# Running the output projection, LayerNorm and FFN of one query chunk inside the attention of the next, in a pre-norm transformer block

## The chip, the cores and the metric

The kernel runs on one core of a Trainium2 chip. The metric is device time in microseconds (us) of one execution. Runs marked "one look" have one time, no interval and a state that is on record as unknown; they are read by stretches of their traces.

Engines are named as the profile names them: PE (matmul), PEld (weight load of PE), ACT (activations), DVE (vector), SP (which issues the loads). "Granted clock" is the share of full speed at which PE was clocked. PSUM is the memory that matmuls write their sums to, in eight banks. PV is the product of the exps of the scores with V.

## The reference

```python
x = A_x                                     # 1 x 2048 x 1024, bf16
h = x + attention(layernorm(x), wqkv) @ wo  # 32 heads of 32, full softmax over 2048 keys
out = h + (gelu(layernorm(h) @ w1 + b1) @ w2 + b2)   # w1: 1024 x 3584, w2: 3584 x 1024
```

## The kernel before

A small planner records every operation with the buffers that it reads and writes, and turns them into semaphore waits. Each engine runs its own list strictly in the order of recording. So the order in which Python records the operations is the order on PE, and an operation that has to wait holds back all behind it.

The kernel has three stages, one after the other: LayerNorm with the Q, K and V projections; attention for all four query chunks of 512; then the output projection (Wo), the second LayerNorm and the FFN for all four chunks.

Attention handles one *unit* per exp: two heads of a group of four, one key tile of 128. Cut to its core:

```python
def stage_A(hu):       # scores: two matmuls with 32 rows each, side by side in the array
    for j in range(2):
        pe(matmul(sT[:, s, j, :], KT[32*hl:32*hl+32, g, keys], QT[32*hl:32*hl+32, g, queries],
                  tile_position=(32*hl, 0)))
def stage_B(hu):       # one exp on ACT over both: 128 x 1024
    act(activation(PT[:, ps], sT[:, s], Exp, bias=..., scale=SCALE))
def stage_C(hu1):      # every second unit: 4 PV and 4 denominator matmuls, 32 columns each
    for hl in range(4): pe(matmul(OTp[32*hl:32*hl+32, oi], Vsb[...], PT[...], tile_position=(0, 32*hl)))
    for hl in range(4): pe(matmul(DENp[32*hl:32*hl+32, oi], ones32, PT[...], tile_position=(0, 32*hl)))

LA = NSTP              # 2: score tiles in PSUM, so two units of lookahead
for hu in range(NHU):
    if hu + LA < NHU:
        stage_A(hu + LA); stage_B(hu + LA)
    if hu % 2 == 1:
        stage_C(hu)
        if last_key_tile: finish_group(qc, g)    # reciprocal of DENp, times OTp
```

`[... the projections, the third stage with eight PSUM banks, W2 streamed once per chunk, all cut]`

## Time and profile before

The median is 1943.18 us (4 runs, 1941.04 to 1944.95).

| stage | us of the span | what bounds it |
|---|---|---|
| LayerNorm 1, projections | 0 to 248 | PE, clock 0.96 |
| attention, 4 chunks of 277 us | 248 to 1358 | ACT, with PE nearly full at clock 0.50 |
| Wo, LayerNorm 2, FFN | 1358 to 1939 | PE, clock 0.90, and gaps |

First, lines of the page of the kernel before. The digits are busy tenths in 40 slices of the span; PEclk is the granted clock in the same slices. The two groups name the tile written and read, the shapes, the count, then busy time, the mean of one in ns, and the idle time before them.

```profile
span 1939.2 us, 24118 instructions
PE   4889989999999999999999999999489789779798
ACT  3433389999999999999999999999246045054060
PEclk9999955555555555555555555555689889889899
...
L527 ACT ACTIVATE PT<-sT,biasm 128x1024 bf16<-128x1024 f32 x1024 | 1058.0, 1110 | 51.1 <-PE sT L516 51.1
L516 PE MATMUL sT<-QT,KT 32*128 32x512 bf16 x2048 | 593.4, 603 | 54.8 <-ACT PT L527 54.1
```

ACT idles 51 us in 1024 exps, so the exps set the pace of attention; PE, at half clock, idles little more (55 us at its score matmuls). The clock falls to half at the start of attention and stays there.

Next, four stretches of the kernel before: length, busy time of each engine with the count of instructions, then the granted clock, the share of the DMA engines and GB/s.

```profile
core 0: us, PE busy (x) PEld busy (x) DVE busy (x) ACT busy (x) POOL busy (x), PEclk, DMA share, GB/s
0.00:248.00 248.00, 202.60 (x964) 92.28 (x964) 116.12 (x285) 91.99 (x134) 1.04 (x9) 0.96 0.37 119
248.00:525.00 277.00, 261.58 (x1520) 43.85 (x1524) 28.35 (x14) 264.36 (x257) 0.00 (x0) 0.51 0.00 1
525.00:1358.00 833.00, 794.05 (x4616) 132.63 (x4608) 97.20 (x48) 794.52 (x770) 0.00 (x0) 0.50 0.00 1
1358.00:1939.00 581.00, 478.98 (x2216) 215.73 (x2216) 265.58 (x502) 196.47 (x301) 0.00 (x0) 0.90 0.39 120
```

In the last 581 us ACT works 196 us. Last, PE's instructions in order of time within attention: start, length, then what it is. One period of two exps goes from 801.46 to 803.47, 2.01 us; the next takes 2.32 us, with a wait of 0.20 us for an exp, and so on in turn, which makes the mean of 2.17 us. "x4" at 802.97 is two score pairs in a row, the second at 803.47.

```profile
801.46 0.61 PE L516 MATMUL sT<-QT,KT 32*128 32x512 bf16 x2 [0.20 <-ACT PT L527]
802.00 0.62 PE L544 MATMUL OTp<-PT,Vsb 128*32 128x512 bf16 x4
802.40 0.64 PE L552 MATMUL DENp<-PT,ones 128*32 128x512 bf16 x4
802.97 1.11 PE L516 MATMUL sT<-QT,KT 32*128 32x512 bf16 x4
```

Tiled matmuls that start together occupy PE for one *slot*: 0.40 us from PV to denominators. From a score pair to PV the distance is 0.54 us and from the denominators to a score pair 0.57 us. Those two steps change the tiling of the array (32-row tiles to 32-column tiles and back); PV to denominators doesn't.

### The profile page before, as it was taken

Reading aid. Unit: us, or ns where it says so; the run is one execution under the profiler, and the core shown is the slowest. Engines: PE = TensorE matmul, PEld = TensorE weight load, DVE = VectorE, ACT = ScalarE, POOL = GpSimd, SP = SyncE. Lnnn points to the kernel's source line nnn. Section 1 sums busy time; section 2 is a strip of 40 time slices with the busy share of each in tenths; the row PEclk is TensorE's granted clock in tenths of the full one; section 3 lists DMA queues with packets and bytes.
Section 4 is the critical chain, followed back from the end, with each engine's and each line's share of the span. In section 5 each row is a group of like instructions: output and inputs, shape, how many; then the busy total and the mean of one; then the engine's idle time right before and its main releaser. Section 6 shows DMA issues by size and latency. Waiting matters only on the chain.

```text
span 1939.2 us, 24118 instructions
## 1 busy us (share of the span) xinstructions
PE 1737.2 (90%) x9312; PEld 484.5 (25%) x9312; DVE 507.2 (26%) x849; ACT 1347.3 (69%) x1458; POOL 1.0 (0%) x9
## 2 busy tenths in 40 slices
PE   4889989999999999999999999999489789779798
PEld 2344411111111111111111111111134334334343
DVE  5443500010100101001010010100356156165281
ACT  3433389999999999999999999999246045054060
POOL 0000000000000000000000000000000000000000
PEclk9999955555555555555555555555689889889899
DMA  4343200000000000000000000000422433523434
GB/s 112 130 150 122 95 1 1 1 1 1 1 1 1 1 1 1 1 1 1 1 1 1 1 1 1 1 1 1 152 66 77 150 121 93 173 82 109 155 127 131
DMA packets 84176, 100.13 MB, mean 52 GB/s; under 512 B 7265, under 2 KB 64609, under 8 KB 84066
## 3 DMA queue, kind: packets, MB, share of 16 engines
q1 hardware_dynamic: 84066, 98.59, 16.2%
q8 instruction: 78, 1.28, 0.3%
q14 instruction: 32, 0.26, 0.0%
HBM read 94.38 MB, written 4.19 MB: 51 GB/s over the span
## 4 chain that ended last, share of the span: by engine, by line
PE 60%; ACT 18%; issue 15%; DVE 4%; DMA 2%; ACTq 0%; SPq 0%; DVEq 0%
PE sT L516 15%; ACT PT L527 15%; PE pb L731 10%; PE pb L701 9%; PE OTp L544 7%; PE DENp L552 6%; PE psq L390 6%; PE pb L656 3%; PE psv L435 3%; ACT xnb L336 1%; DVE l3stats L316 1%; DVE ost L746 1%; DMA w1st<-in_B_w_dram 1%; PE pn L410 1%; ACT xnT L347 1%
## 5 line engine op out<-in xcount | busy, mean ns | idle before, releaser
L527 ACT ACTIVATE PT<-sT,biasm 128x1024 bf16<-128x1024 f32 x1024 | 1058.0, 1110 | 51.1 <-PE sT L516 51.1
L516 PE MATMUL sT<-QT,KT 32*128 32x512 bf16 x2048 | 593.4, 603 | 54.8 <-ACT PT L527 54.1
L563 DVE RECIPROCAL rdenf<-DENp 128x512 f32<-128x512 f32 x32 | 107.5, 3358 | 991.0 <-PE DENp L552 991.0
L552 PE MATMUL DENp<-PT,ones 128*32 128x512 bf16 x2048 | 328.6, 633 | 0.0
L544 PE MATMUL OTp<-PT,Vsb 128*32 128x512 bf16 x2048 | 315.4, 608 | 0.4 <-ACT PT L527 0.4
L516 PEld LDWEIGHTS sT<-QT,KT 32*128 32x128 bf16 x2048 | 105.0, 99 | 710.6 <-ACT PT L527 709.5
L706 ACT ACTIVATE xh<-pb,b1half 128x512 bf16<-128x512 f32 x112 | 76.9, 686 | 244.1 <-PE pb L701 243.9
L701 PE MATMUL pb<-hnT,w1st 128*128 128x512 bf16 x896 | 211.5, 397 | 34.9 <-DMA w1st<-in_B_w_dram 33.7
L731 PE MATMUL pb<-w2st,gT 128*128 128x512 bf16 x896 | 194.4, 379 | 0.0
L390 PE MATMUL psq<-xnT,wst 128*128 128x512 bf16 x512 | 129.6, 401 | 4.8 <-ACT l1y L326 2.4
L701 PEld LDWEIGHTS pb<-hnT,w1st 128*128 128x128 bf16 x896 | 90.4, 102 | 148.6 <-DMA w1st<-in_B_w_dram 35.1
L731 PEld LDWEIGHTS pb<-w2st,gT 128*128 128x128 bf16 x896 | 87.5, 98 | 106.2 <-issue 1.2
L544 PEld LDWEIGHTS OTp<-PT,Vsb 128*32 128x32 bf16 x2048 | 57.3, 102 | 224.5 <-issue 223.2
L711 DVE SCALAR_TENSOR_TENSOR uu<-sqf,xh 128x512 bf16<-128x512 bf16 x112 | 77.5, 692 | 3.8
L687 DVE SCALAR_TENSOR_TENSOR gT<-th,xh 128x512 bf16<-128x512 bf16 x112 | 76.7, 685 | 3.5 <-ACT th L685 3.2
L685 ACT ACTIVATE th<-uu 128x512 bf16<-128x512 bf16 x112 | 69.7, 622 | 3.6 <-DVE uu L711 2.8
L656 PE MATMUL pb<-Wo,OT 128*128 128x512 bf16 x256 | 59.8, 390 | 13.1 <-DMA Wo<-in_A_wo_dram 13.1
L390 PEld LDWEIGHTS psq<-xnT,wst 128*128 128x128 bf16 x512 | 52.1, 102 | 71.8 <-issue 18.3
L746 DVE TENSOR_TENSOR ost<-pb,hch 128x512 bf16<-128x512 f32 x32 | 19.9, 684 | 188.2 <-PE pb L737 188.0
L709 DVE TENSOR_TENSOR sqf<-xh 128x512 bf16<-128x512 bf16 x112 | 47.6, 425 | 64.0 <-ACT xh L706 63.7
L552 PEld LDWEIGHTS DENp<-PT,ones 128*32 128x32 bf16 x2048 | 64.0, 114 | 0.0
L435 PE MATMUL psv<-wst,xnT 128*128 128x512 bf16 x256 | 55.9, 379 | 0.0
(66 smaller groups left out, 490.5 us busy)
## 6 DMA issues: line engine op xcount, KB each, us to landing
w1st<-in_B_w_dram SPq DMA_DIRECT2D x28, 1024.0 KB, 5.5
w2st<-in_B_w_dram SPq DMA_DIRECT2D x112, 256.0 KB, 2.6
wst<-in_A_wqkv_dram SPq DMA_DIRECT2D x24, 1024.0 KB, 5.0
xring<-in_A_x_dram SPq DMA_DIRECT2D x32, 256.0 KB, 4.0
out_dram<-ost SPq DMA_DIRECT2D x32, 128.0 KB, 1.7
Wo<-in_A_wo_dram SPq DMA_DIRECT2D x1, 2048.0 KB, 8.4
b2row<-in_B_b_dram SPq DMA_DIRECT2D x1, 2.0 KB
b1col_bf<-in_B_b_dram SPq DMA_DIRECT2D x1, 7.0 KB, 4.6
```

The source lines that it names most:

```text
L390: pe(lambda p, dc=dc, b=b, s=s, cin=cin, xt=xt: p.matmul(psq[:, b, :], wst[:, s, dc, cin:cin + P], xnT[:, xt, dc, :], start=(dc == 0), sto ...
L435: pe(lambda p, dc=dc, t4=t4, s=s, pvs=pvs, xt=xt: p.matmul(psv[:, pvs, 0:OB], xnT[:, xt, dc, t4 * P:(t4 + 1) * P], wst[:, s, dc, :], start ...
L516: pe(lambda p, s=s, j=j, kt=kt, g=g, hl=hl, qc=qc: p.matmul(sT[:, s, j, :], KT[32 * hl:32 * hl + 32, g, kt * P:(kt + 1) * P], QT[32 * hl:3 ...
L527: act(lambda a, s=s, ps=ps, g=g, qc=qc: a.activation(PT[:, ps, :, :], sT[:, s, :, :], ACT.Exp, bias=biasm[:, g, qc:qc + 1], scale=SCALE), ...
L544: pe(lambda p, j=j, kt=kt, g=g, hl=hl, ps=ps, start=start, stop=stop, oi=oi: p.matmul(OTp[32 * hl:32 * hl + 32, oi, :], Vsb[:, kt, g * P + ...
L552: pe(lambda p, j=j, hl=hl, ps=ps, start=start, stop=stop, oi=oi: p.matmul(DENp[32 * hl:32 * hl + 32, oi, :], ones32[:, :], PT[:, ps, j, :] ...
L563: dve(lambda v, rs=rs, oi=oi: v.reciprocal(rdenf[:, rs, :], DENp[:, oi, :]), reads=[B_DENp[oi]], writes=[B_rdenf[rs]])
L656: pe(lambda p, sa=sa, g=g, qc=qc, t4=t4, j=j: p.matmul(pb[:, sa, 0:OB], OT[:, qc, g, t4 * P:(t4 + 1) * P], Wo[:, g, j * OB:(j + 1) * OB], ...
L701: pe(lambda p, hb=hb, s=s, dc=dc, f4=f4, hn=hn: p.matmul(pb[:, hb, :], w1st[:, s, dc, f4 * P:(f4 + 1) * P], hnT[:, hn, dc, :], start=(dc = ...
L706: act(lambda a, gs=gs, hb=hb, fc=fc: a.activation(xh[:, gs, :], pb[:, hb, :], ACT.Identity, bias=b1half[:, fc:fc + 1], scale=0.5), reads=[ ...
L711: dve(lambda v, gs=gs: v.scalar_tensor_tensor(uu[:, gs, :], sqf[:, gs, :], C1, xh[:, gs, :], ALU.add, ALU.mult), reads=[B_sqf[gs], B_xh[gs ...
L731: pe(lambda p, ci=ci, fc=fc, t4=t4, j=j, s2=s2: p.matmul(pb[:, ci, 0:OB], gT[:, fc, t4 * P:(t4 + 1) * P], w2st[:, s2, j * OB:(j + 1) * OB] ...
```

## The change

The intent is to fill PE's and ACT's unlike loads into one another. The post-attention work of chunk c-1 becomes a generator that yields after about four full 128x512 matmuls (a *slice*; 140 steps a chunk), and the attention loop of chunk c takes a step after 3 of every 5 units. The work of the last chunk has no attention to hide in; it is the *tail*. The rest makes room:

- Q goes out to HBM and comes back one chunk at a time.
- All weights of the post work go through one ring of three 1 MB slots, and PSUM keeps two banks (pbA, pbB) for all the post work. So FFN2 takes two outputs at a time and W2 is streamed four times per chunk.
- Evictions of Wo and FFN1 and the normalization move from ACT to DVE.
- PV and denominators have one bank each in place of two; DVE copies them out before the reciprocal.
- GELU buffers shrink from three to two.
- Buffers track which addresses they reuse, in place of a wait for everything so far.

The cut below is condensed: lines are shortened to their sense.

```diff
+        def post_gen(qc):                      # Wo, LN, transposes, FFN1, FFN2 of one chunk
+            srcs += [(W2 block b) for _ in range(4) for b in range(FC // 4)]     # streamed 4 times
+            ...
+                    for g in range(G):
+                        pe(... pw[:, 0:OB], OT[...], wring[...])                 # Wo into pbA / pbB
+                        if g == G // 2 - 1:
+                            yield
+                    dve(lambda v: v.tensor_copy(attb[:, ab, :], pw[:, 0:OB]))    # was act(... Copy)
+                    ...
+                    dve(lambda v: v.tensor_scalar(xh, pw, 0.5, b1half, MULT, ADD))  # was act(Identity)
+            for ci in range(0, len(combos), 2):                                  # FFN2, 2 banks
+                for fc in range(FC):
+                    ... 2 matmuls ...
+                    if fc % 2 == 1:
+                        yield
+        for qc in range(NCH):
+            for _ in attention_gen(qc):
+                i += 1
+                if post is not None and i % 5 in (0, 2, 4):
+                    next(post)                  # (StopIteration handled)
+            post = post_gen(qc)
-        # attention of all chunks, then:
-        for qc in range(NCH):
-            ffn1_gen(qc) woven with wo_ln_gen(qc + 1)
-            ffn2_plan(qc)                       # 8 PSUM banks, W2 streamed once
```

`[... Q through HBM, buffer tracking, group end: cut]`

## The prediction

> **What bounds it now.** The 40-slice picture shows three stages. LayerNorm and projections take 248 us. Attention runs from 248 to 1358 us (1110 us, 277 us per query chunk). Output projection, LayerNorm and FFN take the last 580 us. In attention the groups view gives 1024 exps of 1.03 us issue spacing (ACT about 95% busy, 51 us idle in all): ACT bounds it. PE also looks 95% busy there, but at granted clock 0.50. In the timeline one period of two exps lasts 2.01 us, in which PE streams four slots (two score pairs, four column-tiled PV, four column-tiled denominator matmuls) of about 0.43 us: 1.7 us. In the last stage PE does 512 full 128x512 matmuls per chunk (plus transposes and bias) at clock 0.91, at 0.216 us each (16 in 3.45 us in the chain of waits), so 110 us per chunk; the rest is LayerNorm, load and eviction gaps. ACT is under 40% busy there.
>
> **What the change does.** It runs the post-attention work of chunk c-1 inside the attention of chunk c, about 140 slices of four full matmuls among 256 exps. Only chunk 3's post work remains as a tail. To make room Q goes through HBM, W2 is streamed four times per chunk (29 MB instead of 7), PSUM accumulators shrink to two banks, and the Wo and FFN1 evictions and the normalization go from ACT to DVE. Denominator and output are copied out by DVE (2 x about 0.69 us per group) before the 3.36 us reciprocal.
>
> **Costing a hidden chunk (estimates).** ACT: 277 us + 28 tanh x 0.62 + 4 hnT copies x 1.02 + 2 table loads x 1.28 = 301 us; with stalls at group boundaries and slice waits about 313 us. The Trainium skill ("ScalarE: Activation LUTs", Table sets) puts exp and tanh in one set, so tanh should not reload; the trace has no exp-tanh alternation to show it. DVE: about 150 us, hidden. DMA: in FFN2 1 MB per about 3.7 us, 285 GB/s; W1 bursts reached 350-380 GB/s here, so it just fits. PE: 110 us post + 128 x 0.86 = 220 us at full clock: fits under ACT. At half clock 219 + 219 us plus mode switches, about 460-480 us: PE would bound.
>
> So the clock decides. The skill ("TensorE: Matmul & The Clock Gate", Part 1) says the clock gate opens on activity, half or full. Here attention stayed at 0.50 for 1100 us after a 2 us gap, while full matmuls opened it within about 5 us. I expect dense full-array slices to open it (about 75-80%), with cold stretches around LayerNorm steps.
>
> **Tail.** Wo 15, LayerNorm 10, transposes 8, FFN1 about 70 (DVE-bound: 0.69+0.43+0.69+0.69 = 2.5 us per block of 8 matmuls), FFN2 about 90 (DMA-bound: 29 MB at about 330 GB/s), ends 7: 200 us.
>
> **Sum.** 248 + 277 + 3 x 313 + 200 = 1664, say 1665 us; range 1600 to 1980. Of the roughly 580 us at the end, about 415 go into attention, which grows by about 110; the tail costs 60 more than a quarter of before. Chances: faster 0.82, same 0.04, slower 0.14.
>
> **What would show it.** Granted clock: 0.5 in the first attention chunk, near 1.0 in chunks 1 to 3; ACT about 90% busy there; exp idle under 15%; no table load per tanh; chunks of about 313 us; a tail of about 200 us with FFN2 waiting on weight loads; W2 traffic about 118 MB.
>
> **What would make it wrong.** The clock stays at 0.5 in the mixed chunks: 460+ us each, total about 2100 us. Or W2 loads block PE in order and so starve exp. Or tanh reloads tables (2 x 1.28 us x 28 per chunk). Or DVE copies at group ends stall the single output bank for several us, 32 times.

## The result, and the profile after

The changed kernel takes 1696.27 us (median of 8 runs, 1691.83 to 1702.17), with an output that passed the comparison (e3_quarter shows what that is worth). The ratio to the kernel before is 0.8733 (95% interval 0.8722 to 0.8744). Ratios in this document are of fast runs of the same rounds, so not quite the ratio of the medians that are quoted.

Lines of the page of the changed kernel, as those of before:

```profile
span 1690.4 us, 24078 instructions
PE   4898889999999899999988999999899999957666
ACT  4334349999998899888988998888899988922200
PEclk9999995555556799999787999996799999779998
...
L654 ACT ACTIVATE PT<-sT,biasm 128x1024 bf16<-128x1024 f32 x1024 | 1074.6, 1117 | 89.3 <-PE sT L643 86.0
L643 PE MATMUL sT<-QTc,KT 32*128 32x512 bf16 x2048 | 447.1, 461 | 66.6 <-ACT PT L654 64.8
```

PEclk is at half in the first attention chunk, then mostly open. A chunk with post work in it is called *mixed* below. Exps idle 89 us in place of 51. The stretches of the changed kernel, cut at the ends of the attention chunks:

```profile
core 0: us, PE busy (x) PEld busy (x) DVE busy (x) ACT busy (x) POOL busy (x), PEclk, DMA share, GB/s
0.00:248.00 248.00, 201.91 (x964) 92.22 (x964) 116.14 (x285) 92.64 (x134) 1.05 (x9) 0.96 0.45 145
248.00:525.00 277.00, 262.23 (x1524) 44.44 (x1524) 37.34 (x28) 264.36 (x257) 0.00 (x0) 0.50 0.04 13
525.00:845.00 320.00, 297.55 (x2104) 82.75 (x2100) 135.11 (x193) 287.93 (x292) 0.00 (x0) 0.92 0.41 132
845.00:1165.00 320.00, 297.76 (x2092) 82.75 (x2088) 135.08 (x193) 287.70 (x291) 0.00 (x0) 0.92 0.41 132
1165.00:1484.00 319.00, 297.64 (x2094) 82.78 (x2091) 135.47 (x194) 289.06 (x292) 0.00 (x0) 0.92 0.40 129
1484.00:1690.00 206.00, 137.60 (x552) 52.44 (x550) 97.42 (x165) 23.22 (x34) 0.00 (x0) 0.91 0.55 182
```

So 581 us of post work turned into about 42 us in each of three chunks and a tail of 206 us. A finer ruler is used from here on: attention ends a *group* of four heads (32 exps) with a DVE copy of its output, and the time between two such copies is the time of a group. A group alone takes 34.7 us in both kernels. In the first mixed chunk the eight take:

| group | 1 | 2 | 3 | 4 | 5 | 6 | 7 | 8 |
|---|---|---|---|---|---|---|---|---|
| post work in it | Wo | LayerNorm, transposes, FFN1 | FFN1 | FFN1 | FFN1, FFN2 | FFN2 | FFN2 | FFN2, none |
| us | 41.3 | 46.0 | 40.4 | 37.4 | 42.0 | 38.0 | 38.1 | 35.4 |

How the clock opened can be seen on PE, in order of time, at the first slice of the first mixed chunk:

```profile
530.83 1.89 PE L751 MATMUL pbA<-wring,OT 128*128 128x512 bf16 x4
532.65 0.56 PE L643 MATMUL sT<-QTc,KT 32*128 32x512 bf16 x4
533.14 0.40 PE L670 MATMUL OTp<-PT,Vsb 128*32 128x512 bf16 x4
533.37 0.39 PE L678 MATMUL DENp<-PT,ones 128*32 128x512 bf16 x4
533.69 1.04 PE L751 MATMUL pbA<-wring,OT 128*128 128x512 bf16 x4
```

The first slice of four took 1.89 us at half clock, the second 1.04 us at full clock; by the clock record it opened at 533.0 us, 2.2 us after the first slice began. In all traces here the recorded clock changes only in steps of about 3.4 us, so such delays are coarse. And this is PE in the FFN2 part of the same chunk:

```profile
715.41 0.39 PE L643 MATMUL sT<-QTc,KT 32*128 32x512 bf16 x2
715.73 0.39 PE L823 MATMUL pbA<-wring,gT 128*128 128x512 bf16 x1
715.96 0.38 PE L823 MATMUL pbB<-wring,gT 128*128 128x512 bf16 x1
...
716.39 0.38 PE L823 MATMUL pbB<-wring,gT 128*128 128x512 bf16 x1
716.70 0.39 PE L643 MATMUL sT<-QTc,KT 32*128 32x512 bf16 x2
717.02 0.40 PE L670 MATMUL OTp<-PT,Vsb 128*32 128x512 bf16 x4
717.25 0.39 PE L678 MATMUL DENp<-PT,ones 128*32 128x512 bf16 x4
717.57 0.39 PE L643 MATMUL sT<-QTc,KT 32*128 32x512 bf16 x2
```

Read the distances of the starts, not the lengths, which include the way through the pipeline. Between matmuls of one tiling it is 0.22 us (715.73 to 715.96; 717.02 to 717.25). Where the tiling changes (score pair to full, full to score pair, score pair to PV, denominators to score pair) it is 0.31 or 0.32 us. Each change costs PE about 0.10 us at full clock, and somewhat more at half clock (0.54 to 0.57 in place of 0.40 from PV to denominators and 0.40 to 0.43 between the full matmuls of the slice at 530.83). The Trainium skill ("TensorEngine Tiling (Array Packing)", Key Properties) says that changing the tiling mode drains the engine; it has no figure, and this is one for this kernel. That a drain is the whole of the 0.10 us is not shown.

### The profile page after: what moved, and what is told of

Same layout as the page of the kernel before. It is cut to its first block, busy times and chain, and to the rows that moved or that the text cites. A ratio compares the mean times of both kernels' runs of the same rounds, so it can differ in the third digit from the quotient of the medians.

```text
span 1690.4 us, 24078 instructions
## 1 busy us (share of the span) xinstructions
PE 1494.7 (88%) x9312; PEld 437.4 (26%) x9312; DVE 656.6 (39%) x1057; ACT 1244.9 (74%) x1298; POOL 1.0 (0%) x9
## 4 chain that ended last, share of the span: by engine, by line
PE 61%; ACT 13%; DVE 11%; issue 10%; DMA 4%; ACTq 0%; DVEq 0%; SPq 0%
PE sT L643 16%; ACT PT L654 11%; PE OTp L670 8%; PE psq L472 6%; PE DENp L678 5%; PE pbA L823 5%; PE pbB L823 5%; PE pbB L792 4%; PE pbA L792 4%; DMA wring<-in_B_w_dram 3%; PE psv L525 3%; DVE rdenf L690 2%; DVE xh L800 2%; DVE uu L805 2%; PE pbA L751 2%
## 5 line engine op out<-in xcount | busy, mean ns | idle before, releaser
L643 PE MATMUL sT<-QTc,KT 32*128 32x512 bf16 x2048 | 447.1, 461 | 66.6 <-ACT PT L654 64.8
L670 PE MATMUL OTp<-PT,Vsb 128*32 128x512 bf16 x2048 | 243.7, 466 | 4.4 <-DVE OT L688 2.5
L678 PE MATMUL DENp<-PT,ones 128*32 128x512 bf16 x2048 | 244.8, 468 | 0.3
L643 PEld LDWEIGHTS sT<-QTc,KT 32*128 32x128 bf16 x2048 | 95.5, 94 | 536.2 <-ACT PT L654 397.3
L823 PE MATMUL pbA<-wring,gT 128*128 128x512 bf16 x448 | 178.6, 399 | 32.0 <-DMA wring<-in_B_w_dram 26.2
L823 PE MATMUL pbB<-wring,gT 128*128 128x512 bf16 x448 | 177.0, 395 | 2.1 <-DVE ost L843 2.1
L792 PE MATMUL pbB<-hnT,wring 128*128 128x512 bf16 x448 | 116.6, 389 | 9.7 <-DVE xh L800 8.4
L792 PE MATMUL pbA<-hnT,wring 128*128 128x512 bf16 x448 | 114.4, 383 | 9.1 <-DVE xh L800 9.1
L690 DVE RECIPROCAL rdenf<-rdenf 128x512 f32<-128x512 f32 x32 | 107.3, 3353 | 1.1
L823 PEld LDWEIGHTS pbA<-wring,gT 128*128 128x128 bf16 x448 | 44.6, 100 | 132.9 <-issue 56.7
L800 DVE TENSOR_SCALAR xh<-pbA,b1half 128x512 bf16<-128x512 f32 x56 | 42.0, 750 | 44.7 <-PE pbA L792 42.6
```

What stands on the lines that cost most here:

```text
L643: pe(lambda p, s=s, j=j, kt=kt, g=g, hl=hl, qsl=qsl: p.matmul(sT[:, s, j, :], KT[32 * hl:32 * hl + 32, g, kt * P:(kt + 1) * P], QTc[32 * h ...
L670: pe(lambda p, j=j, kt=kt, g=g, hl=hl, ps=ps, start=start, stop=stop: p.matmul(OTp[32 * hl:32 * hl + 32, :], Vsb[:, kt, g * P + 32 * hl:g ...
L678: pe(lambda p, j=j, hl=hl, ps=ps, start=start, stop=stop: p.matmul(DENp[32 * hl:32 * hl + 32, :], ones32[:, :], PT[:, ps, j, :], start=sta ...
L690: dve(lambda v, rs=rs: v.reciprocal(rdenf[:, rs, :], rdenf[:, rs, :]), reads=[B_rdenf[rs]], writes=[B_rdenf[rs]])
L792: pe(lambda p, s=s, dc=dc, f4=f4, pw=pw: p.matmul(pw[:, :], wring[:, s, dc * 512 + f4 * P:dc * 512 + (f4 + 1) * P], hnT[:, dc, :], start=( ...
L800: dve(lambda v, gs=gs, fc=fc, pw=pw: v.tensor_scalar(xh[:, gs, :], pw[:, :], 0.5, b1half[:, fc:fc + 1], ALU.mult, ALU.add), reads=[Bpw, B_ ...
```

## The experiments

Twelve kernels ran. None of the kernels was refused; there is no run e8 on record.

### e1_serial: the interleaving alone undone (one look)

```diff
-                if post is not None and i % 5 in (0, 2, 4):
+                if False:
```

> The changed kernel with the interleaving alone undone: the post work of each chunk runs after the next chunk's attention, not inside it; everything else of the change stays. Theory O (the gain is the overlap): the projections 248 us, four attention chunks of 277 us at clock 0.5, and four post stretches of about 208 us as the tail of the changed kernel has: about 2190 us, slower than the kernel before, so the rest of the change is a cost that the overlap has to pay back. Rival R (the gain comes from the other edits: work moved from ACT to DVE, fewer waits at the stage borders, weight ring): stays below 1900 us.

Measured: 2192.58 us, against 1940.08 of the kernel before. Attention chunks take 279 us each at clock 0.50, and each post stretch about 210 us. Theory O holds: everything but the overlap is a cost, of about 250 us, and the overlap gives back about 500 us. The rival falls. The post work of chunk 0 and then attention of chunk 2, apart:

```profile
807.00:1017.00 210.00, 137.49 (x549) 52.30 (x556) 97.56 (x165) 23.54 (x35) 0.00 (x0) 0.89 0.55 186
1017.00:1296.00 279.00, 264.08 (x1536) 44.71 (x1534) 37.59 (x29) 265.88 (x257) 0.00 (x0) 0.50 0.04 11
```

### e2_filler: useless slices in attention chunk 0 (one look)

```diff
+                if qc == 0 and i % 5 in (0, 2, 4):
+                    for k_ in range(4):
+                        pe(matmul(pbA or pbB, KT[:, 0, k_*P:(k_+1)*P], KT[:, 0, 0:512]))   # never read
```

> The changed kernel with useless full 128x512 matmuls put into attention chunk 0, four in each of the slots (3 of 5 exps) that the post work has in the later chunks; their result is never read, so the output stays right. They bring no DMA, DVE or ACT work. Theory C (dense full-array slices open the clock gate; the pace of the mixed FFN2 stretch, 1.18 us per exp, is set by PE with its switches between tiled and full matmuls): chunk 0 goes from clock 0.50 to about 1.0 within 10 us, and takes about 256 x 1.18 = 302 us instead of 277, so the whole is about 1720 us. Rival D (the mixed chunks are slow because of weight DMA, DVE or tanh; PE has room): chunk 0 stays at about 277 us or gets faster than that with the faster clock. If the gate doesn't open: about 460 us for chunk 0.

Measured: 1726.73 us. Chunk 0 takes 307 us in place of 279, the mixed chunks 320 as in the changed kernel. This is a stretch well inside chunk 0:

```profile
290.00:540.00 250.00, 236.94 (x1735) 69.71 (x1766) 36.52 (x27) 222.95 (x211) 0.00 (x0) 1.00 0.00 1
```

The clock is open (1.00), there is no load (DMA share 0.00), no tanh, and DVE is nearly idle. Still a group takes 37.5 to 38.8 us, as the FFN2 groups of the mixed chunks do (38.0). So the slices on PE set that pace, not weight loads, DVE or tanh. Theory C holds. An estimate from the steps above shows what the changes of tiling do: ten exps with six slices take 20 tiled slots of 0.22 us, 24 full matmuls of 0.216 us and 19 changes of 0.10 us, or 36.7 us a group, of which 6 us are changes; without them PE would need 31 us and fit under ACT.

### e3_quarter: a quarter of the W2 traffic (one look, wrong)

```diff
-                    dma(wring[:, s_, :]..., ap, ...)
+                    if a == 4:  dma(wring[:, s_, 0:D], ap[:, 0, :], ...)     # W2: first 128 rows of 512
+                    else:       dma(wring[:, s_, :]..., ap, ...)
```

> The changed kernel with each 1 MB load of W2 cut to its first quarter, so the other three quarters of the ring slot are stale: the output is wrong on purpose. W2 traffic falls from about 118 to 29 MB. Theory C (in the mixed chunks the FFN2 stretch is bound by PE, and only the tail's FFN2 by the weight stream): the mixed chunks keep their 315 to 320 us within 3 us, and the tail's FFN2 falls from about 90 us to 50 to 60 us, whole about 1655 us. Rival D (the stream holds the mixed FFN2 stretch back too): the stretch of 122 us falls towards 110 us in each of three chunks, whole about 1620 us.

Measured: 1666.06 us. Mixed chunks: 320, 320 and 321 us, unchanged. The tail falls from 207 to 175 us. So the fourfold stream costs nothing where attention covers it and about 32 us in the tail, as theory C said, though FFN2's end of the tail came to 61 us where 50 to 60 were expected. The waits of the changed kernel's tail show the same: between 1597 and 1690 us PE waits 21 times for a weight block (total, times, longest).

```profile
PE pbA L823 <- DMA wring<-in_B_w_dram: 26.2, 21, 2.2
```

A warning on the side: with three quarters of W2 stale the comparison still called the output right, probably because FFN2's share of the output is small here (`w1` and `w2` are drawn with small factors in the reference). The comparison would not catch an error there.

### e4_dose1: one slice in five slots (one look)

```diff
-                if post is not None and i % 5 in (0, 2, 4):
+                if post is not None and i % 5 == 2:
```

> The changed kernel with post slices in 1 of 5 slots in place of 3 of 5: 51 of about 140 slices are hidden in each of chunks 1 to 3, the other 89 (the last 29 of FFN1's 57 and all of FFN2) run alone afterwards. It asks how dense the full matmuls must be. If the gate opens at this density (clock near 1.0): PE has room, chunk about 285 us plus about 130 us of rest, whole about 248 + 277 + 3 x 415 + 208 = 1980 us. If it stays at 0.5: one period of five exps takes about 5.0 + 1.9 = 6.9 us of PE in place of 5.4, so the hidden part takes about 350 us, whole about 2170 us.

Measured: 2080.05 us, between the two. The hidden part of the first mixed chunk takes about 305 us and the granted clock goes up and down (means of 20 us stretches between 0.50 and 0.95). A slice of four opens the clock at some places and not at others:

```profile
531.69 1.49 PE L751 MATMUL pbA<-wring,OT 128*128 128x512 bf16 x3 [0.33 <-PE DENp L678]
533.11 0.40 PE L643 MATMUL sT<-QTc,KT 32*128 32x512 bf16 x4
...
537.26 1.89 PE L751 MATMUL pbA<-wring,OT 128*128 128x512 bf16 x4
539.08 0.61 PE L643 MATMUL sT<-QTc,KT 32*128 32x512 bf16 x2
```

After the first (one of its four records is missing) a score pair has the length of full clock, 0.40 us; after the second it has that of half clock, 0.61 us, and the clock stayed at half until the next slice, 546.7 us. Of 13 slices that began at half clock in this chunk, two were followed by no opening for 9 us, this one and that of 550.89. Neither pure case holds; slices have to be dense to keep the clock open, and a single one does not open it every time.

### e5_actevict: evictions back on ACT (3 rounds)

```diff
-                    dve(tensor_copy(attb, pw));       dve(tensor_scalar(xh, pw, 0.5, b1half, ...))
+                    act(activation(attb, pw, Copy));  act(activation(xh, pw, Identity, bias=b1half, scale=0.5))
```

> The changed kernel with one part undone: the evictions of the output projection and of FFN1 go back from DVE to ACT. Theory A (ACT is the limit in the Wo and FFN1 stretches of the mixed chunks): 28 x 0.69 + 8 x 0.60 = 24 us more ACT work lengthens each of the three mixed chunks by 20 to 24 us; the tail's FFN1, bound by DVE, gets 15 to 20 us shorter; whole about 1745 us. Rival P (PE is the limit there as in the FFN2 stretch, ACT has room): mixed chunks within 5 us of 318 us, whole about 1680 us.

Measured: 1731.56 us, ratio 0.8903 (0.8888 to 0.8919). Mixed chunks take 332 us, 13 more than in the changed kernel for 24 us of added ACT work; the FFN1 groups 3 and 4 grow from 40.4 and 37.4 to 44.7 and 41.6 us, the FFN2 groups not at all. So ACT's work counts for about half where it falls (between theories A and P), and the move to DVE was worth it. The part of the expectation on the tail failed: FFN1 there took as long as before. e9_tail8act shows why.

### e6_long: slices of eight, half as many (3 rounds)

```diff
-        yield after 4 matmuls;  i % 5 in (0, 2, 4)
+        yield after 8 matmuls;  i % 10 in (0, 4, 7)
```

> The changed kernel with the post work cut into 76 slices of eight full matmuls in place of 140 of four, in 3 of 10 slots, so the same work with half the slices. Theory S (PE binds the FFN2 stretch, and each change between tiled and full matmuls costs it about 0.1 us): about 65 slices fewer save up to 0.2 us each, 10 us per mixed chunk, whole about 1665 us. Rival B (the length of a burst counts: ACT has two score tiles in hand, 2.1 us of exps, and a burst of 1.73 us with what surrounds it outlasts them): exps wait about 0.5 us per slice, 30 us per chunk more, whole about 1790 us.

Measured: 1838.15 us, ratio 0.9456 (0.9433 to 0.9478). Groups take 43 to 50 us. ACT's instructions in order of time in its FFN2 part (in brackets: idle time before, and who ended it):

```profile
759.68 4.13 ACT L654 ACTIVATE PT<-sT,biasm 128x1024 bf16<-128x1024 f32 x4 [1.18 <-PE sT L643]
764.98 3.12 ACT L654 ACTIVATE PT<-sT,biasm 128x1024 bf16<-128x1024 f32 x3 [1.17 <-PE sT L643]
```

Exps wait 1.2 us for each burst of eight, at full clock. The next scores stand behind the burst in PE's order, and two score tiles in hand don't outlast it. Rival B holds for slices of eight; fewer changes of tiling don't pay for it.

### e7_aftercol: slices only after the column-tiled matmuls (3 rounds)

```diff
-                if post is not None and i % 5 in (0, 2, 4):
+                every i % 2 == 0 (after PV and denominators); two steps where i % 20 == 0
```

> The changed kernel with the same 140 slices of four, but each right after the column-tiled matmuls (every second exp, two slices at every twentieth), in place of 3 of 5 slots of both kinds. Theory S (changes of tiling cost PE about 0.1 us each): a slice there adds one change in place of one and a half on the mean, and the load is even: PE needs 2.06 us and ACT about 2.1 us per two exps, so a mixed chunk goes from 318 to about 308 us, whole about 1668 us. Rival B (bursts between two score pairs starve ACT): the burst is now 1.5 us every time, and the whole is not below 1696 us.

Measured: 1720.95 us, ratio 0.8851 (0.8838 to 0.8865): slower than the changed kernel. But the first mixed chunk takes 315.0 us, 3.5 less than before, and only the next two 328 and 330. There the first group takes 53 us in place of 40: the post work now lasts to the end of the chunk, and the load of the next chunk's Q, issued behind it, comes late (PE waits 24.9 us for it in all). The schedule gained a little and a border lost more; as a test of theory S it is clouded. The tail grows too, from 207 to 217 us: there PE waits 12.2 us for the first Wo block.

### e9_tail8act: the tail alone (3 rounds)

```diff
+            nacc = 8 if qc == NCH - 1 else 2        # all PSUM banks are free in the tail
-                     for _ in range(4) ...          # W2 passes
+                     for _ in range(1 if qc == NCH - 1 else 4) ...
+            if qc == NCH - 1:  act(activation(xh, pw, Identity, ...))   else:  dve(...)
```

> The changed kernel with the tail alone altered: for the last chunk, whose post work no attention covers, FFN2 uses all eight PSUM banks (free by then), so W2 is streamed once and not four times, and the FFN1 eviction goes to the idle ACT. Theory T (the tail's FFN2 is bound by the weight stream, its FFN1 by DVE): FFN2 falls from about 90 to about 55 us and FFN1 from 73 to about 52 us, whole about 1640 us. Rival: if the tail's FFN2 is held by the turnover of its banks and PE, and FFN1 by PE, less than 20 us come off.

Measured: 1662.61 us, ratio 0.8549 (0.853 to 0.8568). The tail takes 172 us in place of 207. Nearly all of it comes from FFN2 (59 us from its start to the end, in place of 93). FFN1 still takes 2.5 us per block of eight matmuls. Lines of ACT and then of DVE in the tail of this kernel:

```profile
1563.78 0.69 ACT L801 ACTIVATE xh<-pbA,b1half 128x512 bf16<-128x512 f32 x1 [1.35 <-issue]
1564.36 0.62 ACT L779 ACTIVATE th<-uu 128x512 bf16<-128x512 bf16 x1
```

```profile
1563.01 0.69 DVE L781 SCALAR_TENSOR_TENSOR gT<-th,xh 128x512 bf16<-128x512 bf16 x1
1564.49 0.42 DVE L808 TENSOR_TENSOR sqf<-xh 128x512 bf16<-128x512 bf16 x1 [0.81 <-ACT xh L801]
```

The eviction of the next block starts at 1563.78, just after the last GELU step of the block two before it ends (1563.01 + 0.69 = 1563.70), because they share one of two buffers. If so, the ring of two held FFN1 as soon as DVE's load did not. e10_comb tests that.

### p_pattern: seven patterns of slices in chunk 0 (one look)

```diff
+   n_ = [4 if i % 5 in (0,2,4) else 0, 2, 4 if odd else 0, 4 if even else 0,
+         8 if hu % 4 == 3 else 0, 1, 4 if hu % 4 == 3 else 0, 0][group]     # useless full matmuls
```

> The changed kernel with useless full matmuls in attention chunk 0 alone, in another pattern for each of its eight groups of 32 exps: group 1 four matmuls in 3 of 5 slots (as the post work has them), 2 two after every exp, 3 four after the column-tiled matmuls of every second exp, 4 four between the two score pairs of every second exp, 5 eight at every fourth exp, 6 one after every exp, 7 four at every fourth exp, 8 none. Groups 2 to 5 carry the same 64 matmuls. The known marks: 34.7 us a group with none at clock 0.5, 38.0 with pattern 1. Theory S (PE's occupied time, a matmul slot of 0.216 us and 0.10 us per change of tiling, sets the pace, with ACT's 34 us as the floor): groups 2 to 5 take 35.7, 34, 34, 34 us: many short slices are the slowest. Theory B (the length of a burst ahead of the next score pair sets it, as two score tiles in hand last 2.1 us): group 2 is the fastest of these at about 34.5, groups 3 and 4 about 35 to 36, group 5 over 42 us. Group 6 tells what light use of PE opens the clock, and group 8 whether attention alone holds it open; with a full clock and little else a group may take 33 us.

Measured, with the granted clock inside the group:

| group | pattern | us | clock |
|---|---|---|---|
| 1 | four in 3 of 5 slots | 40.8 (with the start of attention) | opens |
| 2 | two after every exp | 36.6 | 1.0 |
| 3 | four after every second exp's column-tiled matmuls | 35.1 | 1.0 |
| 4 | four between two score pairs | 35.5 | 1.0 |
| 5 | eight at every fourth exp | 47.3 | 0.86 |
| 6 | one after every exp | 33.4 | 1.0 |
| 7 | four at every fourth exp | 39.0 | 0.86 |
| 8 | none | 35.6 | falls to 0.5 |

Theory S has group 2 rightly as the slowest of groups 2 to 4, and its numbers are about 1 to 1.5 us below the measured ones; theory B has groups 3 to 5 right and fails at group 2, which it had as the fastest. So both hold, each on its side of four: short slices cost PE changes of tiling, long ones starve the exps. (One group of each, in one run: groups of one pattern agree within 0.1 us where chunk 0 has no slices, the last group apart, and within 1.3 us in e2_filler.) Group 5 has a second loss: once exps starve, PE idles and the clock falls. Group 7 shows that loss by itself: its slices are as long as those of group 3 and half as many, yet it is 4 us slower, at a clock of 0.86 in place of 1.0. Group 6 has the same 32 matmuls as group 7, spread evenly, and its clock stays open: how the matmuls are spread counts, not only how many there are. Group 6 is the fastest of all: 33.4 us for attention at full clock.

### e10_comb: e9_tail8act with e7's schedule, an early load of Q and three GELU buffers (3 rounds)

```diff
+   slices as in e7_aftercol
+                if hu == NHU // 2 and qc + 1 < NCH:  load_q(qc + 1)
-        NGL = 2
+        NGL = 3
```

> e9_tail8act with three more edits: slices after the column-tiled matmuls only (as e7_aftercol), the next chunk's Q loaded at half of the running chunk in place of at its end (in e7_aftercol exps waited 12 us for it at each of two chunk starts), and three GELU buffers in place of two (in e9_tail8act the ring of two held the tail's FFN1 at 2.5 us per block). Expected: chunks 1 to 3 at 315 us or a little less (the first mixed chunk of e7_aftercol, which had no such wait), the tail's FFN1 from 71 to about 52 us and the tail from 172 to about 153 us: 248 + 279 + 3 x 315 + 153 = 1625 us. If the ring was not what held FFN1, the tail stays at 172 us and the whole at about 1644 us.

Measured: 1652.55 us, ratio 0.851 (0.8497 to 0.8522), the fastest that ran. The tail's FFN1 falls from 71 to 50 us, in which PE is busy throughout: the ring was the cause. The mixed chunks took 314, 326 and 324 us. Q comes in time now, and PE waits for the first Wo block in its place: the ring starts each chunk's post work empty, and the post work before it ends just then. PE first, then ACT, in order of time at the start of the second mixed chunk:

```profile
855.14 1.86 PE L757 MATMUL pbA<-wring,OT 128*128 128x512 bf16 x4 [8.72 <-DMA wring<-in_A_wo_dram]
```

```profile
857.59 2.12 ACT L658 ACTIVATE PT<-sT,biasm 128x1024 bf16<-128x1024 f32 x2 [10.34 <-PE sT L647]
```

Because PE's order is fixed, one slice that waits for a load stops all of attention behind it.

### e11_short: as e10_comb, slices of two (3 rounds)

```diff
-        yield after 4 matmuls
+        yield after 2 matmuls; one step after every exp, two at every sixteenth
```

> As e10_comb, but slices of two full matmuls, one after every exp and two after every sixteenth: about 268 slices per chunk, twice the changes of tiling, half the burst. Theory B (burst length sets the pace): faster than e10_comb, mixed chunks about 305 us, whole about 1597 us. Theory S (PE's occupied time with 0.10 us per change of tiling): slower than e10_comb, FFN2 groups at 36 us or more, whole not below 1635 us.

Measured: 1687.14 us, ratio 0.8676 (0.8654 to 0.8698), slower than e10_comb, as theory S said and theory B did not. The mixed chunks take 332, 340 and 338 us, the first of them, which has no border wait, 17 us more than in e10_comb. But this is not a measurement of changes of tiling. The two groups with FFN2 alone and an open clock grow by 0.1 and 1.2 us (37.2 to 37.3 and 36.8 to 38.0). The 17 us are mostly in group 2 (2.9 us more) and in groups 5 and 8 (6.4 and 6.3 us more), where the clock is at 0.92 in place of 1.0 and, in group 8, PE waits 3.8 us for DVE. What part of this follows from the changes of tiling stays open.

### e12_final: e10_comb with the ring kept full over the border, and one useless matmul per exp in chunk 0 (3 rounds)

```diff
+        srcs = [all blocks of all chunks in one list]; ensure(n) looks past the end of a chunk
+                if qc == 0:
+                    pe(matmul(pbA or pbB, KT[:, 0, 0:P], KT[:, 0, 0:512]))      # after every exp, never read
```

> e10_comb with two edits, each read in its own stretch. First, the weight ring fetches across the border between one chunk's post work and the next, so that the first Wo block is on its way before the last W2 block is used: in e10_comb PE waited 8.7 us for it at the start of chunks 2 and 3, with all the attention behind it. If that wait is the cause, the first groups of chunks 2 and 3 fall from 49 to about 40 us and these chunks from 325 to 315 us. Second, one useless full matmul after every exp of chunk 0, the light pattern of group 6 of p_pattern (33.4 us a group in place of 34.7 with the clock full): chunk 0 from 280 to about 270 us if the clock holds, unchanged if it doesn't open. Together 248 + 270 + 3 x 315 + 158 = 1621 us, the fastest of all; about 1650 us if both fail.

Measured: 1754.6 us, ratio 0.9033 (0.9018 to 0.9048), a failure as a version and the most telling run of all. The first edit did what it should: the first groups of chunks 2 and 3 take 42.5 us in place of 49, these chunks 317 and 319 us, the tail 153 us. The second edit cost 122 us: chunk 0 takes 402 us, 50.1 us a group. Here are 100 us of chunk 0 in e12_final:

```profile
300.00:400.00 100.00, 100.00 (x452) 17.50 (x448) 10.66 (x8) 69.91 (x64) 0.00 (x0) 0.50 0.00 1
```

And here group 6 of p_pattern, which has the same pattern of one matmul after every exp, and then part of group 8:

```profile
445.00:475.00 30.00, 28.49 (x213) 7.54 (x212) 3.61 (x2) 29.61 (x30) 0.00 (x0) 1.00 0.01 1
525.00:545.00 20.00, 19.00 (x116) 3.12 (x108) 0.00 (x0) 19.19 (x20) 0.00 (x0) 0.50 0.00 1
```

The same operations run at 33.4 us a group where the clock was open when they began, and at 50.1 us where it was half: there PE is busy in 100 of 100 us by the record and the clock never opens, in 400 us. In these runs the light pattern holds the clock open and doesn't open it; slices of four in 3 of 5 slots opened it 2 to 5 us after the first of them (2.2, 4.6 and 1.7 us in the three mixed chunks of the changed kernel). I had read group 6 as "this opens the clock", though it had only been seen to keep it open.

e10_comb with the first edit alone was not run; from e12_final's time less the 122 us of chunk 0 it is estimated at 1632 us. That stays an estimate.

## Why the prediction was right

The time was 1696 us against 1665 us predicted, inside the range of 1600 to 1980 us, and the mechanism was the one named. Point by point:

- **The overlap is the gain.** Shown by e1_serial: without it the same kernel takes 2193 us.
- **The clock decides.** It was given 75 to 80% to open on dense full-array slices. It did, within one or two slices, and stayed open but for the LayerNorm steps (0.50 between 567 and 584 us), the ends of chunks and a few single steps (700 to 707 us, where FFN2 begins), with a mean of 0.92. What the other outcome costs is shown by e12_final against group 6 of p_pattern: 50.1 against 33.4 us for the same operations. The prediction leant on the Trainium skill ("TensorE: Matmul & The Clock Gate", Part 1: activity opens the gate). The runs agree for full-array slices, and show that PE being busy by the record is not the activity that counts.
- **Attention alone stays at 277 us.** It took 278 to 279 us at clock 0.50.
- **The mixed chunk, "about 313 us".** It took 318 to 320 us, so three of them are 18 us over. The size was close, but one term was mis-sized and another misnamed. "PE: 110 us post + 128 x 0.86 = 220 us at full clock: fits under ACT" left out the changes of tiling, which the prediction had as "mode switches" at half clock only. With 0.10 us each, PE is the limit in the FFN2 groups (38.0 us a group in place of 34.7; e2_filler shows it without any other load). The 12 us of "stalls at group boundaries and slice waits" were partly this. The prediction derives them from nothing, so that they came near is luck. In the first mixed chunk the eight groups exceed 34.7 us by 6.6, 11.3, 5.7, 2.7, 7.3, 3.3, 3.4 and 0.7 us; ACT's work other than exps in them is 2.8, 7.9, 6.5, 5.8, 1.9, 0, 0 and 0 us. So groups 3 and 4 are no longer than ACT's work explains, and the rest, 16 us net, lies in the groups of Wo and LayerNorm, where the clock is partly at half, and in those with FFN2. DVE's copies at the group ends, named as a danger, cost next to nothing: PE waited 2.5 us for them in the whole run.
- **ACT's added 24 us.** Counted in full in the prediction. e5_actevict shows that 24 us of ACT work in the mixed chunk cost 13 us.
- **tanh doesn't reload tables.** Right: the trace has four table loads before exps and one before a tanh (at the start of the tail, after a square root), for 112 tanhs, 84 of them among the exps. The Trainium skill ("ScalarE: Activation LUTs", Table sets) puts both into one set, and its 1283 ns for a load (same page, What ACT_TABLE_LOAD costs) is what the trace has.
- **Weights fit in the FFN2 part.** Right: at 206 to 308 GB/s in stretches of 10 us between 715 and 815 us, and a quarter of the traffic changed nothing there (e3_quarter).
- **The tail, 200 us.** It took 207: 36 us to the end of the transposes (33 predicted), then 77 until FFN2 begins (72 of them from the first to the last FFN1 matmul; 70 predicted), and 93 from there to the end (97). "DVE-bound" for FFN1 was right in the changed kernel (DVE busy for 93% of the time from 1526 to 1597 us), but the cure showed a second limit at the same 2.5 us, the ring of two buffers. "DMA-bound" for FFN2 is shown by e3_quarter and e9_tail8act.

The 32 us by which the time exceeds the sum of 1664 us are 18 in the mixed chunks, 7 in the tail, 1 to 2 in chunk 0, and 6 between the profiled span (1690) and the median of the timed runs.

What stays open: what exactly PE's activity has to be for the clock to open. The runs show that dense slices of four full matmuls did it within 6 us every time in the changed kernel, that slices of four in one of five slots did it at some places and not at others (e4_dose1), that one full matmul between tiled ones did not in 400 us, and that one was enough to keep the clock open over 33 us of group 6; they don't show a threshold.

## What to carry to other kernels

When two stages load different engines, price the overlap on every engine at both clocks, and count changes of tiling as work: 0.1 us each made PE the limit of the FFN2 groups, where it had been priced to fit under ACT. Cut the inserted work to the lookahead that the other stream has in hand; here, of the lengths that were tried, four matmuls was best; slices of two were slower, and eight starved the exps. On an engine with a fixed order every inserted step must find its data there, so fetch across the borders, and where a state depends on what came before it, as the clock does (one pattern, 33.4 or 50.1 us a group), test it from the state in which it will be entered.

## What the Trainium skill lacked or had wrong

- "TensorEngine Tiling (Array Packing)", Key Properties, says that a change of tiling mode drains the engine, without a size. Here each change between row-tiled, column-tiled and full matmuls of 512 columns cost about 0.10 us over the slot at full clock (0.31 to 0.32 in place of 0.22 us), and 0.11 to 0.17 us at half (0.54 to 0.57 in place of 0.40 to 0.43 us).
- "TensorE: Matmul & The Clock Gate", Part 1, describes the open state as reached after about 3.4 us of sustained busy time. Here PE was busy for 100% of 400 us by the record, with row-tiled, column-tiled and single full matmuls in turn, and the granted clock stayed at 0.50; attention alone, with PE busy for 95%, did so for 1100 us. Slices of four full matmuls opened it 1.7 to 4.6 us after the first one's start in the changed kernel; in e4_dose1 two slices of 13 were followed by no opening for 9 us.
- The same page gives a busy window for opening and an idle one for closing, and tells of kernels that swing between the two states; it doesn't say that one and the same load can hold an open clock open and yet fail to open a closed one: here one full matmul per exp kept an open clock open (33.4 us a group, clock 1.0) and did not open a half-closed one (50.1 us, clock 0.50).
